# Attention and two feed-forward layers on one core: the opening's hand-written order is replaced, and one product goes to the other PSUM bank

## The chip, the core and the metric

The kernel runs on one core of a Trainium2 chip. The metric is the device time of one execution in microseconds (us); of several runs the median is taken. The core has five engines, each with its own queue of instructions that it works off in order: TensorE (PE; its weight loads stand in the profile as PEld), VectorE (DVE), ScalarE (ACT), GpSimd (POOL) and SyncE (SP), which here only issues DMA transfers.

## What is computed

Three stages, all in float32:

```python
for c in range(24):                                # chunks of 32 queries, 4 batches x 8 heads, head width 64
    k_full = concat(mem_k, k[16 before ... 8 after])   # 8 + 56 keys
    scores = scale * (q_c @ k_full.T)
    a = exp(scores - max); a = a / (sum(a) + 1e-9)
    out[:, :, c] = a @ v_full
x = out as 3072 tokens x 512
h = x @ w_in                                       # 512 x 2048
x = (relu(h) ** 2) @ w_out                         # 2048 x 512
return (silu(x @ w_gate) * (x @ w_val)) @ w_out2   # 512 x 1536 twice, 1536 x 512
```

## The kernel before

**Units and blocks.** Attention is cut into 24 units of 128 queries (4 chunks) with all 8 heads. Four units make a block of 512 tokens, and the first feed-forward layer runs over six such blocks, 16 slices f of its 2048 inner columns in each. For each block and f, PE makes 12 matmuls of the hidden product (L362, from x and w into one of the two PSUM banks `hbank`), ACT and DVE turn them into the squared relu, split into a high part gh and a low part gl, and PE makes 12 matmuls of the projection (L406, into four banks `yb`). The second layer follows with a fast matrix product scheme (L596, L643). Nothing of that is touched.

**The opening.** Until the main loop starts at f = 14 of the first block, the order of all engines is written out by hand: the string `OPENING` is a list of tokens, a letter and a number, and the loop after L760 calls the letter's function with the number. A token may issue instructions on several engines. Since each engine works in order, the sequence of the tokens sets the order in each engine's queue, that of SP's loads too. Waits between engines come from the tiles that the instructions share. The letters that the text below uses, u being a unit and f a slice of weights:

| token | function | engine | what it does |
|---|---|---|---|
| Q u, V u, L f | `at_load`, `at_load_v`, `load1` | SP | load q and k (592 KB), v (512 KB for units 0 to 3), weights (1024 KB) |
| S u | `at_scores` L150 | PE | 32 small score matmuls into bank `yb` (even u) or `abank` (odd u) |
| M, D, A, I, N u | L162, L169, L179, L233/L234, L183 | DVE | max, subtract, sum, reciprocal, scale |
| E u | `at_exp_0` L175 | ACT | exponential |
| T u | `at_turn_0` L189 | PE | 4 transposes of the probabilities |
| C u | `at_turned_0` L192 | ACT | copies them out of PSUM |
| O u | `at_pv_0` L204 | PE | 32 small matmuls, product with v, into `hbank` |
| X u, Y u | L281, L285 | ACT, DVE | high and low part of the unit's 128 columns of x, read from `hbank` |
| p, z or s, j, h, l f | L331, L340 or L335, L345, L349, L353 | ACT, ACT or DVE, DVE, ACT, DVE | turn the loaded weights into a high and a low part |
| x0, y0, w0, v0 | L362 | PE | hidden product of slice 0: x0, y0, w0 for units 0 to 2 (384 columns), v0 for unit 3 |
| a, b f; c, d f | L362; L406 | PE | hidden product; projection |
| Z n | `stir` L753 | PE | n matmuls of a zero tile (`calm`) into `hbank[0]`; nobody reads their result |

The units 0 to 3 have a way of their own (the functions that end in `_0`): there the product with v writes four 128-column pieces into one bank of `hbank`,

```python
o = hbank[1][:, 0:KD * GQ].rearrange("p (j q) -> p j q", q=GQ)
```

so that the product of the next unit (O of u+1) waits until X and Y of unit u have read that bank. x0 writes `hbank[0]` and needs X of units 0, 1 and 2. SP has eight semaphores for its transfers and gives them out in turn, so that the ninth load waits until the first has landed.

Of the kernel before, what the change touches and what calls it, by code (L numbers as in the profile page):

```python
# [20 lines left out]
GQ = NC * CHUNK  # L21
# [5 lines left out]
KD = DM // 128  # L27
# [29 lines left out]
WC = 1024  # L57
EARLY = (1, 2, 3, 4)
OPENING = """
Q0 Z9 S0 M0 D0 Q1 Z1 S1 M1 D1 Q2 Z1 S2 E0 A0 I0 N0 Z7 T0 E1 C0 A1 I1 N1 Q3 S3 L0 p0 T1 C1 M2 D2 M3 D3 E2 A2 I2 V0 Z2 O0 X0 L2  # L60
Y0 V1 Z2 O1 z0 N2 j0 L1 p2 Z6 T2 E3 A3 V2 z2 X1 I3 Y1 N3 C2 s1 p1 Z2 O2 j1 h0 Z4 T3 V3 X2 x0 Y2 C3 O3 l0 j2 y0 h1 L4 p4 X3
h2 l1 Q4 S4 w0 Y3 v0 z4 L3 a1 b1 L5 L6 M4 F4 r0 l2 j4 a2 p3 s3 j3 b2 q0 r1 L7 t0 s5 g0 L8 G4 K4 c0 h3 d0 q1 l3
h4 l4 a3 b3 c1 t1 g1 U4 z6 r2 Q5 p5 j5 s7 q2 V4 p6 t2 r3 h5 L9 q3 d1 a4 L15 b4 c2 g2 d2 a5 j6 r4 l5 t3 g3 b5
W4 c3 s9 h6 l6 p7 j7 L11 d3 O4 s15 p8 z8 j8 r5 S5 M5 L10 q4 q5 a6 p9 b6 c4 t4 g4 d4 h7 l7 a7 t5 L13 g5 b7 c5
F5 j9 h8 l8 G5 r6 K5 d5 a8 X4 b8 Y4 U5 q6 c6 Q6 r7 t6 V5 g6 W5 S6 p10 z10 j10 h9 s11 d6 q7 r8 t7 a9 q8 p11 l9
h10 O5 g7 M6 t8 j11 L12 X5 l10 b9 F6 h11 V6 Y5 G6 g8 c7 l11 d7 a10 K6 U6 b10 r9 z12 q9 p12 j12 t9 g9 c8 d8 p13
a11 W6 s13 b11 c9 d9 L14 r10 O6 z14 h12 Q7 l12 j13 S7 M7 r11 q10 Q8 p14 t10 g10 q11 t11 g11 h13 F7 G7 a12 j14
h14 b12 c10 r12 q12 l13 K7 X6 d10 a13 t12 b13 c11 d11 l14 U7 r13 q13 g12 t13 a14 b14 c12 p15 d12 r14 Y6 q14 W7
j15 h15 V7 O7 S8 t14 a15 X7 l15 b15 g13 c13 M8 Y7 d13 r15 q15 t15 g15 F8 g14
"""  # L70


# [1 line left out]
def attention_moe_moe_kernel(ctx, tc, att, av, v0, w1, w2, out):  # L74
# [19 lines left out]
    hbank = [ps.tile([128, 512], F32, name=f"hbank{i}") for i in range(2)]  # L94
# [99 lines left out]
    def at_pv_0(u):  # L194
        s = st[u]
        v = s["v"].rearrange("p (c j d) -> p c j d", c=NC, d=D)
        o = hbank[1][:, 0:KD * GQ].rearrange("p (j q) -> p j q", q=GQ)
        s["o"] = o.rearrange("p (r i) q -> p r i q", r=2)
        for j in range(NI):
            for c in range(NC):  # L200
                q = slice(32 * c, 32 * c + 32)
                for b in range(2):
                    half = slice(D * b, D * b + D)
                    pe.matmul(  # L204
                        o[half, j, q], v[half, c, j], first_t[u % 2][half, j, q],
                        start=True, stop=True, tile_position=(D * b, D * b),
                    )
# [362 lines left out]
    s3 = []  # L570
# [281 lines left out]
    for k in range(2):  # L852
# [7 lines left out]
        o = acc["x"][:, k:k + 1]  # L860
# [75 lines left out]
```

## Time and profile before

| | us |
|---|---|
| median of 3 runs | 1118.83 (1118.21 to 1119.39) |
| the profiled execution | 1117.84 |
| its span, first to last instruction | 1115.9 |
| around the span | 1.94 |
| PE busy | 1107.7 (99% of the span) |
| DVE, ACT, POOL busy | 657.5, 505.7, 315.9 |
| first projection matmul (c0, L406) starts | 40.65 |

Times inside an execution are counted from the start of its span. In a row of the timeline stand start, length, engine, line, operation, what is written and read, and how many instructions were merged; in square brackets the idle time of the engine before it and what ended it ("issue": nothing that the profile shows). A 32-matmul token has 64 records on PE, since each small float32 matmul is two. PE's clock has two levels, 1.2 and 2.4 GHz; the column PEclk is the granted share of the higher.

### The profile page before, as it was taken

The numbers are of one execution on the slowest core, as the hardware profiler recorded it, in microseconds if no ns is written. First come the engines' busy times: TensorE is split into PE (matmuls) and PEld (weight loads), VectorE is DVE, ScalarE is ACT, GpSimd is POOL, SyncE is SP. The second block draws the span as 40 slices with busy tenths as digits, with TensorE's granted clock in tenths as the row PEclk, the third lists the DMA queues.
The fourth block names the chain that finished last, engine by engine and source line by source line (L and its number), as shares of the span: only waits on it lengthen the run. The fifth ranks groups of instructions, "written<-read, shape, count | busy, mean of one in ns | idle before, by whom it ended". The sixth has DMA issues, their size and how long they took to land.

```text
span 1115.9 us, 17938 instructions
## 1 busy us (share of the span) xinstructions
PE 1107.7 (99%) x7066; PEld 913.5 (82%) x7066; DVE 657.5 (59%) x956; ACT 505.7 (45%) x1026; POOL 315.9 (28%) x261
## 2 busy tenths in 40 slices
PE   8999999999999999999999999999999999999998
PEld 6888888888888888888888888888888888888887
DVE  6879454555454454441523666796666697666664
ACT  4878556556656645553542221452222352222242
POOL 0000025315522521450000332451332461333251
PEclk9999999999999999999999999999999999999999
DMA  9923156656664644634225564457556567655751
GB/s 381 369 78 107 52 201 226 204 206 206 217 219 159 195 153 159 224 127 143 76 76 205 211 231 158 162 210 258 189 205 247 193 208 245 201 200 197 264 208 57
DMA packets 69203, 212.83 MB, mean 191 GB/s; under 512 B 5376, under 2 KB 37632, under 8 KB 52864
## 3 DMA queue, kind: packets, MB, share of 16 engines
q1 hardware_dynamic: 69120, 211.70, 54.4%
q8 instruction: 55, 0.90, 0.3%
q14 instruction: 28, 0.23, 0.1%
HBM read 166.07 MB, written 45.61 MB: 190 GB/s over the span
## 4 chain that ended last, share of the span: by engine, by line
PE 98%; DVE 2%; issue 0%; ACT 0%; DVEq 0%; ACTq 0%
PE yb L406 24%; PE hbank L362 24%; PE hbank L596 15%; PE yb L596 15%; PE yb L643 7%; PE abank L643 7%; PE abank L265 2%; PE abank L150 1%; PE hbank L753 1%; PE hbank L643 1%; PE hbank L204 1%; DVE ring L104 0%; DVE first_p L169 0%; DVE first_p L183 0%; DVE mx L162 0%; DVE sm L179 0%
## 5 line engine op out<-in xcount | busy, mean ns | idle before, releaser
L362 PE MATMUL hbank<-x,w 128*128 128x512 f32 (+2 forms) x1164 | 278.4, 388 | 0.0
L362 PEld LDWEIGHTS hbank<-x,w 128*128 128x128 f32 x1164 | 217.0, 188 | 44.6
L387 DVE TENSOR_TENSOR gl<-r,gh 128x512 fp32r<-128x512 f32 x96 | 75.7, 791 | 246.9 <-ACT r L381 246.8
L406 PE MATMUL yb<-gh,w 128*128 128x512 f32 x768 | 194.7, 392 | 0.0
L406 PEld LDWEIGHTS yb<-gh,w 128*128 128x128 f32 x768 | 142.9, 188 | 30.5
L104 POOL TENSOR_TENSOR ring<-uf,ring 128x512 fp32r<-128x512 f32 x51 | 72.5, 1422 | 294.8 <-ACT ring L101 293.1
L596 PE MATMUL hbank<-w,wst 128*128 128x512 f32 x540 | 132.6, 389 | 0.0
L596 PE MATMUL yb<-w,wst 128*128 128x512 f32 x540 | 132.6, 389 | 0.0
L370 ACT ACTIVATE r<-hbank 128x512 f32<-128x512 f32 x96 | 57.5, 599 | 158.9 <-PE hbank L362 158.9
L461 POOL TENSOR_TENSOR wraw<-cut 128x256 f32<-128x256 f32 x36 | 26.5, 737 | 337.8 <-DVE cut L447 285.4
L596 PEld LDWEIGHTS yb<-w,wst 128*128 128x128 f32 x540 | 101.4, 188 | 21.1
L596 PEld LDWEIGHTS hbank<-w,wst 128*128 128x128 f32 x540 | 101.4, 188 | 21.0
L406 PE MATMUL yb<-gl,w 128*128 128x512 f32 x384 | 105.7, 389 | 0.0
L634 ACT ACTIVATE tmp<-tmp 128x512 f32<-128x512 f32 x36 | 22.8, 632 | 169.4 <-DVE tmp L633 169.4
L583 POOL TENSOR_TENSOR uf<-uf 128x512 f32<-128x512 f32 x36 | 53.9, 1498 | 121.2 <-DVE uf L635 108.0
L101 ACT CAST ring<-uf 128x512 fp32r<-128x512 f32 x108 | 67.0, 621 | 46.1 <-PE yb L643 21.3
L406 PEld LDWEIGHTS yb<-gl,w 128*128 128x128 f32 x384 | 72.0, 188 | 15.0
L643 PE MATMUL yb<-ring,wst 128*128 128x512 f32 x360 | 83.3, 389 | 0.4 <-DVE sum L674 0.4
L643 PE MATMUL abank<-ring,wst 128*128 128x512 f32 x360 | 83.3, 389 | 0.1
L643 PEld LDWEIGHTS yb<-ring,wst 128*128 128x128 f32 x360 | 67.5, 188 | 14.8 <-ACT w L101 0.8
L643 PEld LDWEIGHTS abank<-ring,wst 128*128 128x128 f32 x360 | 67.5, 188 | 14.5 <-issue 0.5
L248 DVE STREAM_TRANSPOSE pT<-prob 32x256 f32<-32x256 f32 x160 | 69.6, 435 | 2.3
(134 smaller groups left out, 1446.1 us busy)
## 6 DMA issues: line engine op xcount, KB each, us to landing
wst<-w2d SPq DMA_DIRECT2D x93, 1024.0 KB, 4.9
wraw<-in_w_dram SPq DMA_DIRECT2D x34, 1024.0 KB, 9.0
w2d<-wraw SPq DMA_DIRECT2D x48, 256.0 KB, 2.5
qk<-in_att_dram SPq DMA_DIRECT2D x20, 592.0 KB, 6.1
v<-in_av_dram SPq DMA_DIRECT2D x20, 384.0 KB, 5.6
y1d<-ys SPq DMA_DIRECT2D x6, 1024.0 KB, 5.3
w2d<-wraw SPq DMA_DIRECT2D x12, 512.0 KB, 3.4
zraw<-y1d SPq DMA_DIRECT2D x6, 1024.0 KB, 7.6
```

The source lines that it names most:

```text
L101: act.copy(hi, src)
L104: lo_engine.tensor_tensor(lo, src, hi.bitcast(F32), ALU.subtract)
L248: dve.transpose(pT[row + k:row + k + 32, pair, :, row:row + 32], probs[u % 2][32 * c:32 * c + 32, :, k:k + 32],)
L362: pe.matmul(hbank[f % 2][:, cols], wt[:, k * 128:(k + 1) * 128], x[:, k, cols], start=i == 0, stop=i == 3 * KD - 1,)
L370: act.activation(r, hbank[f % 2][:, 0:n], AF.Relu)
L387: dve.tensor_tensor(gl, g["r"], g["gh"].bitcast(F32), ALU.subtract)
L406: pe.matmul(ybank[e][:, 0:nt_of[t]], wt[:, c:c + 128], gtile[t, f][g], start=f == 0 and p == 0, stop=f == NF1 - 1 and p == 2,)
L461: pool.tensor_tensor(o, x, y, op)
L583: pool.tensor_tensor(u_of(p, o), u_of(p, x), u_of(p, y), op)
L596: pe.matmul(to, wt[:, k * 128:k * 128 + 128], x[:, k], start=m == 0, stop=m == 5)
L634: act.activation(u4, u4, AF.Silu)
L643: pe.matmul(to[k], wt[:, 128 * k:128 * k + 128], u, start=p == 0 and m == 0, stop=p == NP - 1 and m == 2,)
```

## The change

The string `OPENING` is written anew, in one sequence for all engines, and `at_pv_0` puts the product of unit 1 into `hbank[0]`. Of the zero-tile matmuls 24 are left of 34. The core of the diff (of the string, its first two lines):

```diff
 OPENING = """
-Q0 Z9 S0 M0 D0 Q1 Z1 S1 M1 D1 Q2 Z1 S2 E0 A0 I0 N0 Z7 T0 E1 C0 A1 I1 N1 Q3 S3 L0 p0 T1 C1 M2 D2 M3 D3 E2 A2 I2 V0 Z2 O0 X0 L2
-Y0 V1 Z2 O1 z0 N2 j0 L1 p2 Z6 T2 E3 A3 V2 z2 X1 I3 Y1 N3 C2 s1 p1 Z2 O2 j1 h0 Z4 T3 V3 X2 x0 Y2 C3 O3 l0 j2 y0 h1 L4 p4 X3
...
+Q0 Z9 S0 M0 Q1 V0 Q3 Q2 S1 Z6 M1 D0 S2 E0 D1 A0 I0 E1 A1 N0 I1 M2 N1 L0 S3 T0 p0 Z2 T1 D2 M3 E2 C0 D3 A2 Z3 O0 z0
+X0 j0 I2 N2 Y0 V1 L2 Q4 L1 V2 V3 p2 C1 Z4 T2 S4 O1 E3 A3 I3 N3 h0 C2 p1 X1 s1 j1 Y1 T3 O2 C3 X2 x0 Y2 z2 h1 O3
...
@@
     def at_pv_0(u):
         s = st[u]
         v = s["v"].rearrange("p (c j d) -> p c j d", c=NC, d=D)
-        o = hbank[1][:, 0:KD * GQ].rearrange("p (j q) -> p j q", q=GQ)
+        o = hbank[int(u != 1)][:, 0:KD * GQ].rearrange("p (j q) -> p j q", q=GQ)
```

On PE, from the scores of unit 1 on. `hbank_74` and `hbank_75` are `hbank[0]` and `hbank[1]`, `yb_77` and `abank` hold scores, `yb_78` and `yb_79` the transposes of even and odd units. Before:

```order
L753 MATMUL hbank_74<-calm 128x512
L150 MATMUL yb_77<-early 32x64 x32
L753 MATMUL hbank_74<-calm 128x512 x7
L189 MATMUL yb_78<-eye,first_p 128x128 x4
L150 MATMUL abank<-early 32x64 x32
L189 MATMUL yb_79<-eye,first_p 128x128 x4
L753 MATMUL hbank_74<-calm 128x512 x2
L204 MATMUL hbank_75<-first_p,first_v 64x32 x32
L753 MATMUL hbank_74<-calm 128x512 x2
L204 MATMUL hbank_75<-first_p,first_v 64x32 x32
L753 MATMUL hbank_74<-calm 128x512 x6
L189 MATMUL yb_78<-eye,first_p 128x128 x4
```

Now:

```order
L753 MATMUL hbank_74<-calm 128x512 x6
L150 MATMUL yb_77<-early 32x64 x32
L150 MATMUL abank<-early 32x64 x32
L189 MATMUL yb_78<-eye,first_p 128x128 x4
L753 MATMUL hbank_74<-calm 128x512 x2
L189 MATMUL yb_79<-eye,first_p 128x128 x4
L753 MATMUL hbank_74<-calm 128x512 x3
L204 MATMUL hbank_75<-first_p,first_v 64x32 x32
L753 MATMUL hbank_74<-calm 128x512 x4
L189 MATMUL yb_78<-eye,first_p 128x128 x4
L150 MATMUL abank<-early 32x64 x32
L204 MATMUL hbank_74<-first_p,first_v 64x32 x32
```

The scores of units 2 and 3 now stand side by side ahead of the first transposes; the transposes of unit 2 and the scores of unit 4 stand ahead of the product of unit 1, which goes to the other bank; and from there to O3 no zero-tile matmul is left.

On ACT, from the two first exponentials on. Before:

```order
L175 ACTIVATE first_p<-first_p 128x512 x2
L192 COPY first_p<-yb_78 128x512
L331 ACTIVATE wraw<-wraw 128x1024
L192 COPY first_p<-yb_79 128x512
L175 ACTIVATE first_p<-first_p 128x512
L281 CAST x_339<-hbank_75 128x4x128
```

Now:

```order
L175 ACTIVATE first_p<-first_p 128x512 x2
L331 ACTIVATE wraw<-wraw 128x1024
L175 ACTIVATE first_p<-first_p 128x512
L192 COPY first_p<-yb_78 128x512
L340 ACTIVATE wraw<-wraw 128x1024
L281 CAST x_337<-hbank_75 128x4x128
```

C0, the copy that O0 waits for (L192 from `yb_78`), moved behind p0 (L331, which waits for the weights of L0) and E2.

On SP, the first loads (`qk` and `early` are q and k of units 0 to 4, `first_v` is v, `wraw` are weights):

```order
 L129 DMA qk<-in_att_dram 128x1184
-L129 DMA early<-in_att_dram 128x1184 x3
+L129 DMA early<-in_att_dram 128x1184
+L137 DMA first_v<-in_v_dram 128x1024
+L129 DMA early<-in_att_dram 128x1184 x2
 L323 DMA wraw<-in_w_dram 128x2048
 L137 DMA first_v<-in_v_dram 128x1024
 L323 DMA wraw<-in_w_dram 128x2048
-L137 DMA first_v<-in_v_dram 128x1024
+L129 DMA early<-in_att_dram 128x1184
```

The v of unit 0 moved from sixth to third place, q and k of unit 2 from third to fifth (the string says Q3 Q2), the first weights from fifth to sixth, q and k of unit 4 from thirteenth to ninth.

## Rows read from the trace of the kernel before

**Rows 1.** The page: busy time and instructions by engine, and one DMA queue.

```profile
PE 1107.7 (99%) x7066; PEld 913.5 (82%) x7066; DVE 657.5 (59%) x956; ACT 505.7 (45%) x1026; POOL 315.9 (28%) x261
...
q8 instruction: 55, 0.90, 0.3%
```

**Rows 2.** Waits of PE from 30 us to the end, longest first.

```profile
PE yb L643 <- DVE sum L674: 0.4, 1, 0.4
```

**Rows 3.** Timeline of PE in the opening.

```profile
7.17 0.86 PE L150 MATMUL abank<-early 64*32 64x64 f32 x64
...
9.45 1.85 PE L753 MATMUL hbank<-calm 128*128 128x512 f32 x7
...
12.46 1.03 PE L150 MATMUL abank<-early 64*32 64x64 f32 x64
...
14.63 2.05 PE L204 MATMUL hbank<-first_p,first_v 64*64 64x32 f32 x64
...
18.68 2.29 PE L204 MATMUL hbank<-first_p,first_v 64*64 64x32 f32 x64 [1.33 <-DVE first_p L183]
20.91 2.93 PE L753 MATMUL hbank<-calm 128*128 128x512 f32 x6
...
28.39 0.94 PE L362 MATMUL hbank<-x,w 128*128 128x384 f32 x4
29.36 2.06 PE L204 MATMUL hbank<-first_p,first_v 64*64 64x32 f32 x64
31.35 0.97 PE L362 MATMUL hbank<-x,w 128*128 128x384 f32 x4
32.25 0.86 PE L150 MATMUL abank<-early 64*32 64x64 f32 x64
33.04 7.77 PE L362 MATMUL hbank<-x,w 128*128 128x384 f32 x40
40.65 1.98 PE L406 MATMUL yb<-gh,w 128*128 128x512 f32 x8
```

**Rows 4.** Timeline of DVE: Y0, then N2.

```profile
17.40 0.65 DVE L285 TENSOR_TENSOR x<-hbank,x 128x512 fp32r<-128x512 f32 x1
17.96 0.68 DVE L183 TENSOR_TENSOR first_p<-first_p,sm 128x512 f32<-128x512 f32 x1
```

**Rows 5.** Busy time in stretches: PE, PEld, DVE, ACT, POOL, then PEclk, DMA share, GB/s.

```profile
0.00:12.52 12.52, 10.20 (x218) 7.24 (x223) 5.83 (x14) 2.75 (x4) 1.62 (x8) 1.00 0.86 333
0.00:17.36 17.36, 14.94 (x350) 10.88 (x350) 10.32 (x25) 6.23 (x10) 1.62 (x8) 1.00 0.91 360
...
17.36:18.64 1.28, 0.00 (x0) 0.00 (x0) 1.28 (x4) 1.28 (x2) 0.00 (x0) 1.00 0.92 384
20.40:23.70 3.30, 3.30 (x19) 2.55 (x17) 2.50 (x6) 1.11 (x2) 0.00 (x0) 0.50 1.03 418
```

**Rows 6.** Timeline of PEld inside the scores of unit 3.

```profile
12.46 0.54 PEld L150 LDWEIGHTS abank<-early 64*32 64x32 f32 x40 [0.17 <-issue]
```

**Rows 7.** DMA queue q8 in two stretches: 10.3:11.4 and 16.2:17.3.

```profile
q8 instruction: 1, 0.02, 5.3%
...
q8 instruction: 1, 0.02, 5.9%
```

**Rows 8.** DMA issues at 0.80 (Q0), 2.19 (Q3), 3.45 (V0): KB, us to landing.

```profile
qk<-in_att_dram SPq DMA_DIRECT2D x1, 592.0 KB, 4.1
...
early<-in_att_dram SPq DMA_DIRECT2D x1, 592.0 KB, 7.0
...
first_v<-in_v_dram SPq DMA_DIRECT2D x1, 512.0 KB, 10.4
```

**Rows 9.** Timeline of ACT: p0, E2, X2.

```profile
13.05 1.16 ACT L331 ACTIVATE wraw<-wraw 128x1024 f32<-128x1024 f32 x1
...
15.02 0.63 ACT L175 ACTIVATE first_p<-first_p 128x512 f32<-128x512 f32 x1 [0.16 <-DVE first_p L169]
...
27.12 0.59 ACT L281 CAST x<-hbank 128x512 fp32r<-128x512 f32 x1 [0.19 <-PE hbank L204]
```

More of the change, by code (lines that the diff above doesn't have):

```diff
@@ L59 @@
 OPENING = """
-Q0 Z9 S0 M0 D0 Q1 Z1 S1 M1 D1 Q2 Z1 S2 E0 A0 I0 N0 Z7 T0 E1 C0 A1 I1 N1 Q3 S3 L0 p0 T1 C1 M2 D2 M3 D3 E2 A2 I2 V0 Z2 O0 X0 L2
-Y0 V1 Z2 O1 z0 N2 j0 L1 p2 Z6 T2 E3 A3 V2 z2 X1 I3 Y1 N3 C2 s1 p1 Z2 O2 j1 h0 Z4 T3 V3 X2 x0 Y2 C3 O3 l0 j2 y0 h1 L4 p4 X3
[L62 to L69, printed above, removed]
+Q0 Z9 S0 M0 Q1 V0 Q3 Q2 S1 Z6 M1 D0 S2 E0 D1 A0 I0 E1 A1 N0 I1 M2 N1 L0 S3 T0 p0 Z2 T1 D2 M3 E2 C0 D3 A2 Z3 O0 z0
+X0 j0 I2 N2 Y0 V1 L2 Q4 L1 V2 V3 p2 C1 Z4 T2 S4 O1 E3 A3 I3 N3 h0 C2 p1 X1 s1 j1 Y1 T3 O2 C3 X2 x0 Y2 z2 h1 O3
+l0 j2 y0 L4 X3 p4 Y3 M4 l1 w0 v0 a1 b1 L3 L7 z4 h2 r0 p3 s3 l2 a2 r1 q0 j3 q1 t0 g0 L8 L5 L6 h3 F4 G4 t1 s7 l3
+s5 j4 b2 c0 h4 p5 r2 d0 a3 b3 c1 K4 g1 Q5 L9 L15 L10 V4 L12 l4 j5 r3 q2 q3 t3 t2 h5 z6 p6 d1 a4 g3 g2 U4 c2 b4
+d2 a5 l5 W4 r4 p8 j6 b5 p7 z8 q4 h6 r5 j7 l6 O4 j8 S5 c3 d3 L13 Q6 c4 a6 h7 q5 t4 g4 s15 M5 s9 F5 l7 d4 a7 b7
+b6 c5 G5 h8 p9 t5 p10 r6 K5 U5 g5 l8 a8 d5 X4 b8 j9 W5 Y4 q6 c6 t6 L11 V5 g6 S6 h9 r7 p11 s11 M6 q7 r8 a9 O5
+d6 t7 z10 F6 j10 l9 h10 q8 g7 j11 L14 Q7 X5 l10 h11 t8 G6 g8 c7 b9 d7 a10 K6 l11 U6 r9 z12 p12 q9 j12 t9 g9 Y5
+W6 s13 b10 c8 d8 r10 a11 b11 c9 h12 p13 q10 z14 V6 l12 j13 S7 O6 r11 p14 t10 q11 h13 t11 g10 M7 F7 G7 a12 d9
+j14 g11 c10 d10 b12 r12 h14 q12 l13 K7 a13 t12 X6 b13 a14 c11 g12 l14 U7 r13 p15 q13 b14 d11 c12 d12 t13 r14
+W7 j15 Y6 q14 h15 V7 Q8 O7 S8 c13 t14 X7 a15 g13 M8 l15 b15 d13 Y7 g14 r15 q15 t15 g15 F8
 """
```

## The prediction

> **What bounds the kernel now.** I read the page first: PE is busy for 1107.7 of 1115.9 us [rows 1], so the time falls only by what PE stands still for, does for nothing, or does at the lower clock. Then PE's waits: from 30 us to the end there are 0.4 us of them [rows 2]. The change can therefore act only in the first 33 us, and one number measures it: when c0, the first projection matmul, starts (40.65 now [rows 3]). Before it PE has the same real work in both orders, and from the matmuls at 33.04 on it has no gap. Third, the timeline of PE up to there [rows 3] against those of DVE and ACT [rows 4, 9]. Last the DMA queues [rows 7, 8], because the loads are reordered too.
>
> Two things in the opening are not what they seem. **O1** is shown as waiting 1.33 us for N2 [rows 3], but it reads nothing of N2; it needs bank 1 free from Y0, which ends at 17.40 + 0.65 = 18.05 [rows 4], and still starts at 18.68. Between 17.36 and 18.64 PE issues no weight load either [rows 5]. Up to there it had issued 350 + 350 = 700 instructions [rows 5]. It stood once before with nothing to wait for, 0.17 us inside the scores of unit 3, which took 1.03 instead of 0.86 [rows 3, 6], after 218 + 223 = 441 [rows 5]. The distance is 259. Queue q8, named "instruction", brings 55 packets of 0.90 MB, one for 2 x 7066 / 55 = 257 PE instructions [rows 1], and a packet ended about 1.3 us before each of the two stands [rows 7]. So I read: PE stood for its code, a block of some 256 instructions at a time, and while the loads fill the DMA engines the block after next comes one trip after PE enters the next one. The trips: the boundary at 441 - 256 = 185 lies 0.25 us into S1 (Z9, S0 and one zero matmul are 148 instructions), at 7.4, and PE went on at 12.7: 5.3 us; from there to 18.65: 5.9 us.
>
> By the Trainium skill, page "Runtime: NRT & Kernel Launch", section "Instruction fetch mechanics", code comes in 16 KiB blocks of 256 instructions, and a block boundary is "mostly hidden". The blocks agree with the rows; the hiding does not, in 17.36 to 18.64.
>
> The other thing is **the clock**: from 20.4 to 23.7 it was at 0.50, 1.2 GHz [rows 5], after the pause and the thin matmuls of O1. Six zero matmuls took 2.93 us there, against 1.85 for seven at the full clock [rows 3].
>
> **The change, part by part.** I lay the new order out with the row durations.
>
> *Loads.* Q0 lands at 4.9, Q3 at 9.2 [rows 8], 1.44 us a load of 592 KB; 512 KB by size 1.25. S1 can go right after S0 at 6.8 (now 7.17, one zero matmul less). Q2 is fifth instead of third, behind V0 and Q3: it lands at 9.2 + 1.25 = 10.5 instead of 7.8, and S2 goes to 10.5 to 11.3. S1 ends at 7.65 and the six zero matmuls (6/7 of 1.85 [rows 3]) at 9.2; 1.3 us of pause remain. S3 follows and is cut by the first code boundary: 185 instructions lie 0.25 us into S1, at 7.05, plus 5.3 is 12.35. S3 ends near 12.9, which is 0.6 earlier than now. L0 comes after the same bytes as V0 does now and lands at 3.45 + 10.4 = 13.85 [rows 8].
>
> *O0.* On ACT, C0 is queued behind p0, which waits for L0, and behind E2: 13.85 + 1.05 + 0.55 + 0.6 (ACT's instructions overlap their neighbours by 0.1) [rows 9] puts its end at 16.0. O0 starts at 16.0 instead of 14.63, with 0.8 us of pause after the three zero matmuls. It takes 2.0 [rows 3], and the four zero matmuls end at 19.1. T2 and S4, which now stands at 32.25, follow by 20.75; DVE has a weight join (j0) queued ahead of the N2 that T2 waits for, and half a us there changes nothing, since the code sets the end of O1, as follows.
>
> *O1, other bank.* It no longer waits for Y0, and O2 no longer for X1 and Y1. x0, which writes that bank, now waits for Y1 as well, but it needs X2 anyhow, which is later. O1 starts at 20.75, and here the code decides. The boundaries after 441 and 700 lie at 956 and 1212. Counted through the new order, 700 falls into the four zero matmuls, 956 into O1 with 12 of its 128 instructions left, at 22.5. The blocks come at 12.35, then 18.3 and 24.3, with 5.9 to 6.0 us a trip. So O1 stands for 1.9 us at its end and is done at 24.6. With the short trip of 5.3 twice it would stand 0.5 us; with half a us more each, 2.9.
>
> *To c0.* T3 0.4; O2 25.05 to 27.05; X2 0.6 [rows 9], a pause of 0.7; x0 at 27.75 instead of 28.39; O3 needs Y2 (0.65 like Y0 [rows 4]) and runs from 28.65 to 30.65 (31.35 now); the next 256 run out 0.4 us before its end, at 30.25, when their block is just due (24.3 + 5.9). y0 takes 0.7, and since S4 (32.25 to 33.04) is already done, the long run of 40 matmuls starts at 31.35 instead of 33.04. **Order alone: -1.7 us.** The ten zero matmuls less cost or give nothing of their own: they lay in pauses, and the pauses that are left (1.3, 0.8, 1.9, 0.7) are longer than now.
>
> *After c0.* The same matmuls follow in another order, 1.7 us earlier. With the row durations no wait of PE comes out up to 130 us; the nearest is 0.2 us of room at the product with v of unit 4, near 78 us. The loads that fill the DMA engines until 50 us are the same bytes. I cost this at 0, with 0.2 to 1 us if that room is gone.
>
> *The clock.* Now no zero matmul stands between 19.1 and x0. The stretch from 20.75 to 27.75 has O1, 1.9 us of stand, O2 and 0.7 us of pause; the stretch ahead of the fall at 20.4 had O0's end, two zero matmuls, 1.3 us of stand and O1. I take one stretch of 3.3 us at 0.50 in it or behind it. Its price lies between 0 (all on pauses) and half of it, 1.65 (all on wide matmuls: 0.26 each at full, 0.49 at half clock [rows 3]). O1 lost 2.29 - 2.05 = 0.24 us with about 0.6 us of it in the low stretch [rows 3, 5], a loss of 0.4 a us. With 2.0 us on O2 or O3, 0.6 on pause and 0.7 on x0 I get 0.8 + 0.3 = **+1.1 us**.
>
> **The sum**: -1.7 + 1.1 = -0.6 us against the profiled execution, 1117.2. The median of the runs is 0.99 above that execution; I let the new one have the same: **1118.2**.
>
> **Rivals.** *One: PE does not stand for code in O1.* Either the trips are as short as the first or my reading of 18.68 is wrong. By that page's rule this is what happens. The sum that follows needs only the rows: O1 ends at 22.75, T3 at 23.2, O2 at 25.2, x0 starts at 25.9, O3 at 26.75, and the 40 matmuls at 29.4: -3.6 us, 1114.2 in the profiled measure, 1115.2 as a median; with one low stretch 1116.3. For it: only two stands show. Against it: both lie 256 instructions apart, and nothing else is due then. Chance 0.17.
>
> *Two: the clock stays down, and the kernel is slower.* With no zero matmuls from 19.1 on, nothing dense comes until 31; now six at half clock stood right behind the fall, and the clock was back at 23.8. If it stays at 0.50 from about 23.7 to 34, three stretches cost 1.1 + 1.1 + 1.65 = 3.85, and -1.7 + 3.85 = +2.1, 1120.9; with code later by 0.5 us a trip, 1.0 us in all, 1121.9. With two stretches, +0.5, 1119.3, it is still no change. It decides from the third stretch on. Chance of three 0.12, of two 0.18.
>
> *Three: the gain is lost behind c0.* Weights or the unit-4 product come as late as before, and PE waits there: 1118.8. Against it: no wait comes out of the durations. Chance 0.08. That the change is not made as told can be left out: the new order stands in the program's queues.
>
> **The numbers.** A difference of 0.2%, 2.24 us, is about what a measurement of this kernel can tell from no change. The forecast (0 or 1 low stretch, 1117.1 to 1118.2) has 0.45. Faster, under 1116.6, are most of rival one and a little of the forecast: 0.18. Slower, over 1121.07, is most of rival two with three stretches: 0.1. The rest, 0.72, is within. The range goes from rival one with a small part of a low stretch, 1115.6, to three stretches, cut a little, 1120.8.
>
> **What would show it.** Right: S2 starts near 10.5; O0 near 16; O1 starts near 20.75 and is drawn out to 3.5 us or more, with a packet on q8 ending 1.3 us ahead of its rest; c0 starts between 39 and 40; one low stretch of the clock between 20 and 31; no wait of PE after 40. Wrong: O1 in 2.1 us (rival one), the clock at 0.50 still at 32 (rival two), or c0 early and a PE wait of a us or more between 40 and 130 (rival three).

## The result, and the profile after

| | before | after |
|---|---|---|
| median (range) of 6 runs each, side by side | 1118.47 (1117.85 to 1119.39) | 1124.34 (1122.98 to 1126.30) |
| the profiled execution | 1117.84 | 1124.26 |
| its span | 1115.9 | 1122.4 |
| c0 starts | 40.65 | 47.10 |
| profiled execution less c0 | 1077.19 | 1077.16 |

The ratio is 1.0053, with a 95% interval of 1.0040 to 1.0066: slower by half a per cent, beyond the range that was given. The last line of the table says where: whatever stands behind c0 takes the same time to 0.03 us, and c0 itself comes 6.45 us late. The waits of PE from 30 us to the end agree; only x0 has one now that it did not have (in the kernel before it ran at 28.39, behind zero matmuls and T3). Behind it stands the one that was there before [rows 2], and no other:

```profile
PE hbank L362 <- ACT x L281: 0.7, 1, 0.7
PE yb L643 <- DVE sum L674: 0.4, 1, 0.4
```

So the view to read is again the timeline of PE in the opening. To be held against [rows 3]:

```profile
7.08 1.66 PE L753 MATMUL hbank<-calm 128*128 128x512 f32 x6
10.39 0.85 PE L150 MATMUL yb<-early 64*32 64x64 f32 x64 [1.65 <-DVE sm L233]
11.04 0.36 PE L150 MATMUL abank<-early 64*32 64x64 f32 x15
12.69 0.97 PE L150 MATMUL abank<-early 64*32 64x64 f32 x49 [1.28 <-issue]
...
16.01 0.95 PE L753 MATMUL hbank<-calm 128*128 128x512 f32 x3
16.89 2.06 PE L204 MATMUL hbank<-first_p,first_v 64*64 64x32 f32 x64
...
20.44 0.86 PE L150 MATMUL abank<-early 64*32 64x64 f32 x64
21.23 1.87 PE L204 MATMUL hbank<-first_p,first_v 64*64 64x32 f32 x57
24.85 0.42 PE L204 MATMUL hbank<-first_p,first_v 64*64 64x32 f32 x7 [1.75 <-issue]
25.20 0.66 PE L189 MATMUL yb<-eye,first_p 128*128 128x128 f32 x4
25.79 3.31 PE L204 MATMUL hbank<-first_p,first_v 64*64 64x32 f32 x64
29.78 1.65 PE L362 MATMUL hbank<-x,w 128*128 128x384 f32 x4 [0.68 <-ACT x L281]
31.36 3.63 PE L204 MATMUL hbank<-first_p,first_v 64*64 64x32 f32 x64
34.92 12.34 PE L362 MATMUL hbank<-x,w 128*128 128x384 f32 x44
47.10 1.98 PE L406 MATMUL yb<-gh,w 128*128 128x512 f32 x8
```

Up to 25 us this is the layout of the prediction. O1 stands for 1.75 us with 57 of its 64 records done, on "issue", which is nothing that the profile shows. Queue q8 had one packet ahead of it (22.3 to 23.5):

```profile
q8 instruction: 1, 0.02, 5.7%
```

Then the same instructions begin to take longer. O3 lasts 3.63 us where it lasted 2.06 [rows 3], x0 1.65 instead of 0.94. The view by stretches gives the reason in its PEclk column (columns as in [rows 5]):

```profile
0.00:12.54 12.54, 8.23 (x222) 6.09 (x223) 6.23 (x17) 2.75 (x4) 1.62 (x8) 1.00 0.85 335
12.54:15.96 3.42, 3.27 (x58) 2.80 (x58) 2.12 (x5) 1.91 (x3) 0.00 (x0) 0.50 1.02 424
15.96:26.20 10.24, 8.49 (x224) 7.23 (x224) 8.08 (x15) 7.35 (x11) 0.00 (x0) 1.00 1.03 419
26.20:43.26 17.06, 16.38 (x154) 15.07 (x151) 9.02 (x11) 8.13 (x10) 0.00 (x0) 0.50 1.01 417
43.26:60.00 16.74, 16.74 (x75) 13.86 (x74) 12.17 (x18) 14.26 (x34) 0.00 (x0) 1.00 0.69 231
```

Before, the granted clock was at 0.50 once, from 20.3 to 23.7. Now it is so from 12.5 to 16.0 and again for 17 us, from 26.2 to 43.3. PE is not idle there: it is busy for 16.38 of 17.06 us. Within that stretch most of the 44 matmuls of the long run, y0 among them, went on at half clock (here the instructions of L362 alone: PE, PEld, then PEclk, DMA share, GB/s; an instruction that runs across a bound is counted on both sides):

```profile
34.92:40.20 5.28, 5.28 (x21) 5.28 (x21) 0.50 1.01 413
40.20:43.26 3.06, 3.06 (x9) 2.38 (x9) 0.50 1.02 423
43.26:47.10 3.84, 3.84 (x18) 2.98 (x16) 1.00 1.04 374
```

They are of three widths (L362 alone, from 34.9 to 47.2): first the eight of y0 and w0 with 384 columns, then the twelve of v0 with 128, then those with 512.

```profile
L362 PE MATMUL hbank<-x,w x44: 308/415/735, 34.9 to 46.9; 128*128 128x512 f32 x24, 128*128 128x128 f32 x12, 128*128 128x384 f32 x8
```

**What the clock cost.** From the start of O2 to c0 the changed kernel took 47.10 - 25.79 = 21.31 us. At the full clock the same work takes: O2 1.99 (as O3 did, 29.36 to 31.35) and the pause for X2 0.68; then from x0 to c0, as before but without S4, 40.65 - 28.39 - (33.04 - 32.25) = 11.47 [rows 3]. Together 14.14. From O2 on the clock cost 7.2 us by this sum. All that stands ahead of O2, the low stretch at 12.5 included, gained the rest, 7.2 - 6.45 = 0.7 us. More than half of the 7.2 us lies in the long run: from 34.92 to c0 it took 12.18 us, where the same 44 matmuls took 0.90 + 7.61 = 8.51 before [rows 3].

### The profile page after: what moved, and what is told of

It is laid out like the page before. It is cut to its first block, busy times and chain, and to the rows that moved or that the text cites. A ratio compares the mean times of both kernels' runs of the same rounds, so it can differ in the third digit from the quotient of the medians.

```text
span 1122.4 us, 17926 instructions
## 1 busy us (share of the span) xinstructions
PE 1111.3 (99%) x7056; PEld 918.3 (82%) x7056; DVE 657.4 (59%) x956; ACT 505.8 (45%) x1026; POOL 316.2 (28%) x261
## 4 chain that ended last, share of the span: by engine, by line
PE 98%; DVE 1%; issue 0%; ACT 0%
PE hbank L362 24%; PE yb L406 24%; PE yb L596 15%; PE hbank L596 15%; PE yb L643 7%; PE abank L643 7%; PE abank L265 2%; PE abank L150 2%; PE hbank L204 1%; PE hbank L643 1%; PE hbank L753 1%; DVE ring L104 0%; PE yb L189 0%; PE yb L150 0%; DVE mx L162 0%
## 5 line engine op out<-in xcount | busy, mean ns | idle before, releaser
L362 PE MATMUL hbank<-x,w 128*128 128x512 f32 (+2 forms) x1164 | 282.8, 393 | 0.7 <-ACT x L281 0.7
L362 PEld LDWEIGHTS hbank<-x,w 128*128 128x128 f32 x1164 | 221.1, 192 | 45.7 <-ACT x L281 0.8
```

Source lines behind the costliest of these rows:

```text
L362: pe.matmul(hbank[f % 2][:, cols], wt[:, k * 128:(k + 1) * 128], x[:, k, cols], start=i == 0, stop=i == 3 * KD - 1,)
```

## The experiments

Theory A: the time went into the clock, which stayed low because from O1 to the long run PE has no zero matmuls any more, only narrow ones, x0 and pauses. Theory B: the order itself (the loads, C0 behind p0 and E2, the stand for code) lost the time, and the clock only shows it. In the diffs a piece of `OPENING` stands alone; B n is a new token, n zero matmuls into `hbank[1]` where Z writes `hbank[0]`. Every kernel was timed beside the kernel before on the same chip (there 1118.94 to 1119.34).

| run | median (range) | ratio [95%] | profiled | c0 | clock at 0.50, 7 us to c0 |
|---|---|---|---|---|---|
| zeros back | 1118.92 (1118.10 to 1119.99) | 0.9995 [0.9985, 1.0004] | 1118.96 | 41.67 | none |
| early zeros only | 1123.64 (1122.85 to 1127.68) | 1.0053 [1.0036, 1.0071] | 1122.85 | 45.75 | 25.5 to 39.1 |
| eight zeros ahead of x0 | 1122.63 (1120.55 to 1123.13) | 1.0031 [1.0019, 1.0042] | 1121.09 | 43.92 | 12.7 to 16.0, 26.4 to 33.1 |
| before, less Z6 | 1120.19 (1118.06 to 1120.92) | 1.0004 [0.9995, 1.0014] | 1119.72 | 42.31 | 20.1 to 30.2 |
| S4 back | 1119.73 (1118.13 to 1120.96) | 1.0005 [0.9996, 1.0014] | 1120.02 | 42.79 | 11.7 to 15.0, 28.7 to 35.5 |
| zeros back, S4 back | 1118.15 (1117.39 to 1120.35) | 0.9992 [0.9983, 1.0001] | 1120.35 | 43.19 | 20.9 to 24.2 |
| bank alone | 1119.04 (1117.97 to 1119.84) | 1.0004 [0.9995, 1.0013] | 1119.11 | 41.91 | 18.1 to 24.8 |
| zeros back, bank undone | 1118.85 (1118.30 to 1128.54) | 1.0014 [0.9996, 1.0033] | 1118.30 | 41.14 | none |
| S4 back, zeros, first | 1118.18 (1117.12 to 1123.68) | 1.0005 [0.9990, 1.0020] | 1117.12 | 39.95 | none |
| S4 back, zeros, second | 1117.37 (1117.07 to 1124.12) | 0.9997 [0.9984, 1.0010] | 1117.17 | 39.97 | none |
| S4 back, zeros, third | 1117.39 (1117.04 to 1118.17) | 0.9983 [0.9974, 0.9993] | 1117.38 | 40.25 | none |

In all of them the profiled execution less c0 is 1077.10 to 1077.41, so c0 is the one number to compare. It differs between executions of one kernel, since the clock does not fall at the same place in each; one profile shows one of them.

### Zero matmuls put back (changed kernel)

```diff
-S1 Z6 M1
+S1 Z11 M1
-Z3 O0
+Z6 O0
-T2 S4 O1 E3
+T2 S4 Z4 O1 B5 E3
-O2 C3 X2 x0
+O2 C3 X2 Z4 x0
```

> The changed kernel with zero-tile matmuls put back into its pauses and nothing else moved: 11 instead of 6 ahead of S2, 6 instead of 3 ahead of O0, 4 ahead of O1, 5 behind O1 (into hbank[1], which is free there), 4 ahead of x0. Theory A (the time went into the clock, which stood at 0.50 from 26.2 to 43.3 because nothing dense stands between 19.9 and 35): no stretch at 0.50 between 7 us and the end, c0 near 40.5 instead of 47.1, and a median of 1117.5 to 1118.5, level with the kernel before. Theory B (the new order, its loads and its stand for code lose the time, and the clock is a side effect): the 18 more matmuls cost 18 x 0.26 = up to 4.7 us where they don't lie in a pause, c0 at 47 or later and 1124 to 1129.

The clock did not fall at all (all engines, then PEclk):

```profile
7.00:41.67 34.67, 31.25 (x565) 26.36 (x549) 24.46 (x43) 20.95 (x29) 0.00 (x0) 1.00 1.02 419
```

Eighteen useless matmuls were added and the 0.5% is gone: 0.9995 instead of 1.0053. Theory B, which had 1124 or more, falls. c0 came 1.2 us later than expected, and the median lies 0.4 us above the expected range. The stand in O1 is still there, shorter because O1 starts later:

```profile
22.57 1.52 PE L204 MATMUL hbank<-first_p,first_v 64*64 64x32 f32 x45
25.07 0.77 PE L204 MATMUL hbank<-first_p,first_v 64*64 64x32 f32 x19 [0.97 <-issue]
```

### More zero matmuls in the early pauses alone (changed kernel)

```diff
-S1 Z6 M1
+S1 Z12 M1
-T0 p0 Z2 T1
+T0 p0 Z4 T1
-Z3 O0
+Z7 O0
```

> The changed kernel with more zero matmuls in the early pauses alone: 12 instead of 6 ahead of S2, 4 instead of 2 between T0 and T1, 7 instead of 3 ahead of O0. From T2 to x0 nothing is added. Theory A: the stretch at 0.50 from 12.5 to 16 goes away, the long one behind O1 stays, because its cause is the stand for code in O1 and the thin work up to x0: c0 45 to 48, 1122 to 1126. If any zero matmuls at all mended it, 1119.

```profile
7.00:25.50 18.50, 14.91 (x359) 12.40 (x359) 15.00 (x32) 9.56 (x13) 0.00 (x0) 1.00 1.02 420
25.50:39.10 13.60, 12.91 (x150) 11.90 (x147) 6.13 (x9) 6.68 (x9) 0.00 (x0) 0.50 1.01 419
```

As theory A has it: the first low stretch is gone, the long one is not, and the ratio is that of the changed kernel. Zero matmuls ahead of O0 do not bring it back; the place that matters lies behind them.

### Eight zero matmuls ahead of x0 (changed kernel)

```diff
-O2 C3 X2 x0
+O2 C3 X2 Z8 x0
```

> The changed kernel with one edit: eight zero matmuls ahead of x0, where PE pauses 0.7 us for X2. At half clock they take about 3.9 us, so 3.2 us of useless work in the way. Theory A (the clock comes back behind dense work, whoever reads it): it comes back at about 33 to 34 instead of 43.3, c0 at 42.5 to 44.5 instead of 47.1, and the time falls by 2 to 4 us against the changed kernel, to 1120 to 1122. Theory B (the clock is a side effect, or dense work does not bring it back): 3.2 us later, 1127 or more.

```profile
24.88 0.42 PE L204 MATMUL hbank<-first_p,first_v 64*64 64x32 f32 x7 [1.85 <-issue]
25.82 3.24 PE L204 MATMUL hbank<-first_p,first_v 64*64 64x32 f32 x64
28.98 3.78 PE L753 MATMUL hbank<-calm 128*128 128x512 f32 x8
32.56 1.13 PE L362 MATMUL hbank<-x,w 128*128 128x384 f32 x4
33.62 2.06 PE L204 MATMUL hbank<-first_p,first_v 64*64 64x32 f32 x64
...
43.92 1.98 PE L406 MATMUL yb<-gh,w 128*128 128x512 f32 x8
```

```profile
26.40:33.10 6.70, 6.70 (x62) 5.86 (x59) 3.29 (x4) 2.75 (x4) 0.00 (x0) 0.50 1.02 421
33.20:43.92 10.72, 10.72 (x112) 9.46 (x111) 5.89 (x8) 7.64 (x11) 0.00 (x0) 1.00 1.02 419
```

The stand in O1 ends where it did (24.88, and 24.85 in the changed kernel), so the zero matmuls are all that differs behind it. The fall is where it was, at 26.4, and 3.8 us of work that nobody reads bring the clock back at 33.1 instead of 43.3. c0 comes 3.2 us earlier than in the changed kernel; the time's interval moves from 1.0040 to 1.0066 down to 1.0019 to 1.0042; the median, 1122.63, is a little above the 1120 to 1122 expected. Theory B expected 3.2 us later.

### The kernel before without Z6

```diff
-L1 p2 Z6 T2
+L1 p2 T2
```

> The kernel before without its six zero matmuls behind O1 (Z6, 20.91 to 23.84 at half clock), nothing else. Theory A: they were what brought the clock back at 23.7; without them it stays at 0.50 beyond 30, c0 at 41 to 45 instead of 40.65 though 2.9 us of useless work are gone, and the median is 1119 to 1123. Theory B: useless work in the way is gone, c0 1 to 1.5 us earlier, 1117 to 1117.5.

```profile
20.10:30.20 10.10, 10.10 (x115) 8.83 (x113) 6.10 (x10) 4.59 (x6) 0.00 (x0) 0.50 1.02 419
```

The converse, in the old order: without its six zero matmuls the low stretch lasts 10.1 us instead of 3.4, and c0 comes at 42.31 although 2.9 us of useless work are gone (O1 started 0.4 us later in this execution, at 19.09). The median lies 0.85 us above that of the kernel before, within what the interval can tell from nothing; theory B's gain of 1 to 1.5 us did not come. The six zero matmuls paid for themselves; that they gave more is not shown.

### S4 back behind y0 (changed kernel)

```diff
-T2 S4 O1
+T2 O1
-y0 L4 X3
+y0 S4 L4 X3
```

> The changed kernel with one token moved: S4 (the scores of unit 4) back behind y0, where the kernel before has it. No zero matmul is added. It moves 128 PE instructions out of the way of O1, so that the 956th falls into O2 or ahead of it and not into O1. Theory of the code stand: O1 runs through in 2.0 to 2.1 us at the full clock, and the stand, what is left of it, moves into T3 or O2 (about 0.5 us or none); the real work up to x0 is 1 to 2 us earlier. Theory A: the pauses stay without dense work, the clock falls again between 20 and 27 and stays at 0.50 for 10 us or more, so 1121 to 1125; were the clock to stay up, c0 would be at 38 and the median at 1116. Theory B: S4 ahead of O1 is the loss, and its move gives 5 us back, 1118 to 1119, with the clock still low.

```profile
19.61 0.85 PE L753 MATMUL hbank<-calm 128*128 128x512 f32 x3 [0.36 <-issue]
20.30 0.60 PE L189 MATMUL yb<-eye,first_p 128*128 128x128 f32 x4
21.01 2.06 PE L204 MATMUL hbank<-first_p,first_v 64*64 64x32 f32 x64
...
24.01 1.70 PE L204 MATMUL hbank<-first_p,first_v 64*64 64x32 f32 x52
26.54 0.54 PE L204 MATMUL hbank<-first_p,first_v 64*64 64x32 f32 x12 [0.82 <-issue]
```

O1 runs through, and the stand has moved on into O2, 12 records from its end: the boundary stays with the count of instructions and not with the token. The clock still falls, but for 6.8 us, from 28.7 to 35.5, and the time is level with the kernel before:

```profile
28.70:35.50 6.80, 6.80 (x135) 6.13 (x135) 3.27 (x4) 4.16 (x6) 0.00 (x0) 0.50 1.01 419
```

That is below the 1121 of theory A and above the 1119 of theory B. So moving S4 alone, without one more zero matmul, took back most of the loss (1.0005 against 1.0053). What it changed is again mostly the length of the low stretch, 6.8 us against 17. Whether the shorter stand (0.82 against 1.75 us) or S4's new place behind y0 did that was not separated.

### The price of the stand: zeros back, S4 back

The first run of this section with the S4 edit of the run above and the same zero matmuls.

> The run with zero matmuls put back (11, 6, 4, 5, 4) and one more edit: S4 behind y0. It prices the stand for code in O1 at the full clock. Theory of the code stand: S4 ahead of O1 costs the stand it makes (0.97 us in that run's trace) and nothing else, since its own 0.8 us are only moved: O1 unbroken at 2.06 us, c0 0.8 to 1.2 us earlier than there (41.67), median 1117.8 to 1118.2. If PE did not stand for code there, moving S4 changes nothing: c0 at 41.7.

The profile fell on the slowest of ten executions, and it cannot give the price: there the code came late for O0,

```profile
16.52 1.87 PE L204 MATMUL hbank<-first_p,first_v 64*64 64x32 f32 x57
19.89 0.42 PE L204 MATMUL hbank<-first_p,first_v 64*64 64x32 f32 x7 [1.50 <-issue]
```

and the clock fell behind it, though O1 ran unbroken (2.06 us). The medians, 1118.15 against 1118.92, differ by 0.8 us the way that was expected, but the intervals of the two ratios overlap (0.9983 to 1.0001 and 0.9985 to 1.0004), so the price of the stand is not shown.

### The bank

In the kernel before, the bank change alone, with the zero matmuls between O1 and O2 sent to the other bank:

```diff
-o = hbank[1][:, 0:KD * GQ].rearrange("p (j q) -> p j q", q=GQ)
+o = hbank[int(u != 1)][:, 0:KD * GQ].rearrange("p (j q) -> p j q", q=GQ)
-p2 Z6 T2
+p2 B6 T2
-p1 Z2 O2
+p1 B2 O2
```

> The kernel before with the bank change alone: the product of unit 1 in hbank[0], and the eight zero matmuls between it and the product of unit 2 in hbank[1], so that they don't wait for its readers. By the reading of the prediction the product of unit 1 stood for code until 18.6, not for the reader of bank 1, which ended at 18.05: it starts at 18.6 to 18.7 as before, c0 within 0.3 us of the kernel before, ratio within 0.9995 to 1.0005. If the bank was what it waited for, it starts 0.6 us earlier.

The reader Y0 of the old bank (DVE), then O1 (PE):

```profile
17.04 0.69 DVE L285 TENSOR_TENSOR x<-hbank,x 128x512 fp32r<-128x512 f32 x1 [0.42 <-ACT x L281]
```

```profile
18.71 3.63 PE L204 MATMUL hbank<-first_p,first_v 64*64 64x32 f32 x64 [1.68 <-ACT wraw L340]
```

O1 starts at 18.71 as before (18.68 [rows 3]), 0.98 us after Y0's end, though it no longer waits for Y0. What the timeline puts the wait down to has nothing to do with O1: a weight tile now, N2 before. Nor was it the v of unit 1, which O1 also reads and which the prediction left out. That load was issued at 4.42 in the kernel before and landed 13.2 us later, at 17.6 (4.49 and 13.1 here):

```profile
first_v<-in_v_dram SPq DMA_DIRECT2D x1, 512.0 KB, 13.2
```

O1 started 1.1 us after that, while S2, where the profile has it wait for its load, started 0.1 us after the landing (11.9 and 12.02 in the run with S4 back). This supports the reading that O1 stood for code. The ratio, 1.0004, has an interval that takes in no change. But c0 came at 41.91, 1.3 us later than in the profile of the kernel before and not within 0.3 as expected: the clock was low for 6.7 us here, against 3.4, and O1 ran in it:

```profile
18.10:24.80 6.70, 6.08 (x70) 5.56 (x71) 4.23 (x8) 3.10 (x4) 0.00 (x0) 0.50 1.02 414
```

The converse, in the kernel with the zeros back (`hbank[1]` again, and Z5 for B5):

> The run with zero matmuls put back (11, 6, 4, 5, 4 of them, S4 left where the change has it), with the bank change undone: the product of unit 1 in hbank[1] again, the five behind it into hbank[0]. The product of unit 2 then waits for X and Y of unit 1, about 1.3 us behind the end of O1 (26.0 + 1.3 = 27.3 in the other run), where it started at 27.57 anyway: both banks come out the same within 0.3 us, 1118 to 1119. If the bank change is worth something here, PE shows a wait of 0.5 us or more at the product of unit 2 and the time goes up by as much.

O2 started at 27.03 with no wait in front of it, behind its T3. Six of ten executions lie between 1118.30 and 1118.86, three at 1120 to 1121, and one at 1128.54 with a mean clock of 0.991, so the interval is wide. A gain from the bank change is not shown.

### A version faster than both

Both edits together, S4 behind y0 and zero matmuls in the pauses, three times with other counts (ahead of S2, between T0 and T1, ahead of O0, behind O0, ahead of O1, behind O1, ahead of x0): 11, 2, 6, 4, 2, 4, 3.

> Both edits: S4 behind y0, and zero matmuls in the pauses (11 ahead of S2, 6 ahead of O0, 2 ahead of O1, 4 behind O1 into hbank[1], 3 ahead of x0). Theory A with the code stand: no stretch at 0.50 between 7 us and the end, no stand of over 1 us inside O1, c0 near 39.0, that is 1.6 us ahead of the kernel before (40.65), and a median of 1116.5 to 1117.3. Theory B: as the run with S4 moved alone, or later by what the added matmuls take.

Seven of the ten executions took 1117.1 to 1118.7, only the fastest of them within the 1116.5 to 1117.3 that was expected of the median; three took 1122.3 to 1123.7 at a mean clock of 0.995 to 0.997. c0 was at 39.95 in the profile, 1 us later than expected. Then 10, 2, 5, 7, 0, 5, 3:

> The version with S4 behind y0 and zero matmuls, their places evened out: 10 ahead of S2, 5 ahead of O0, 7 behind O0 and none ahead of O1, 5 behind O1, 3 ahead of x0. In the earlier version 7 of 10 executions took 1117.1 to 1118.7 and 3 took 1122.3 to 1123.7 with a lower mean clock. [...] Expected: no execution over 1120.5, median 1117.3 to 1118.0, c0 at 39.2 to 39.9, ratio 0.998 to 0.999. [...]

Eight of ten at 1117.1 to 1118.2, but one at 1120.1 and one at 1124.1: the expectation that none would be left was wrong. Then 12, 4, 7, 7, 0, 4, 3:

```diff
-S1 Z6 M1
+S1 Z12 M1
-T0 p0 Z2 T1
+T0 p0 Z4 T1
-Z3 O0
+Z7 O0
-C1 Z4 T2 S4 O1 E3
+C1 Z7 T2 O1 B4 E3
-O2 C3 X2 x0
+O2 C3 X2 Z3 x0
-y0 L4 X3
+y0 S4 L4 X3
```

> The version with S4 behind y0 and zero matmuls in every pause: 12 ahead of S2, 4 between T0 and T1, 7 ahead of O0, 7 behind O0, 4 behind O1, 3 ahead of x0. Two of ten executions of the version with 10, 2, 5, 7, 5, 3 still lost 3 and 7 us to the clock. With the early pauses filled I expect c0 at 39.3 to 40.0 in every execution, the median at 1117.0 to 1117.8, none over 1119.5, ratio 0.998 to 0.999. If executions of 1122 or more remain, the thin matmuls of O0 with their stand are enough by themselves to bring the clock down, and zeros around them don't mend it.

```profile
21.61 2.06 PE L204 MATMUL hbank<-first_p,first_v 64*64 64x32 f32 x64
23.60 1.19 PE L753 MATMUL hbank<-calm 128*128 128x512 f32 x4
24.63 0.60 PE L189 MATMUL yb<-eye,first_p 128*128 128x128 f32 x4
25.15 2.06 PE L204 MATMUL hbank<-first_p,first_v 64*64 64x32 f32 x64
```

```profile
7.00:40.25 33.25, 31.69 (x586) 26.69 (x574) 25.07 (x44) 20.88 (x29) 0.00 (x0) 1.00 1.02 418
```

All ten executions lie between 1117.04 and 1118.17, all at a mean clock of 0.999 or 1.000; the ratio is 0.9983 [0.9974, 0.9993]. From O1 to O2 PE is without a gap; c0, at 40.25, came a little later than the 39.3 to 40.0 expected. It beats the kernel before by 0.17%, where the changed kernel, at 1.0053, lost 0.5%. How much of that is the order and how much the clock is not shown. In the two profiles c0 is only 0.4 us earlier (40.25 against 40.65), with no low stretch here and one of 3.4 us there, while the medians are 1.9 us apart: the kernel before had mean clocks of 0.996 to 0.998 in its executions. The old order with all its pauses filled was not run.

## Why the prediction was wrong, and where it was right

**Right: what measures it.** c0 did measure the whole change: behind it both kernels take 1077.2 us, and no wait of PE was added after 40 us, so rival three falls.

**Right: the loads and the code.** S2 started at 10.39 (forecast 10.5). S3 was cut by the first boundary and went on at 12.69 (12.35). O1 started at 21.23 (20.75); its block came at 24.85 (24.3), with 7 of 64 records left (forecast 12 of 128 instructions, which is 6 records); the stand was 1.75 us (1.9). Rival one falls with it. By the Trainium skill, page "Runtime: NRT & Kernel Launch", section "Instruction fetch mechanics", a boundary is "mostly hidden". While the loads fill the DMA engines (a share of 1.03 from 16.0 to 26.2), it is not: 1.28 and 1.75 us in this one execution, and 0.97, 0.82 and 1.50 us in others above. That it follows the count of instructions was shown by moving S4. One row was misread on the way: the 0.17 us in brackets in [rows 6] lie ahead of the scores, and that as much was lost inside them follows only from 1.03 against 0.86.

**Short: the order alone.** Forecast -1.7, and -0.7 is what is left once the clock's 7.2 us are taken out. 0.74 us of the difference is that O2 started at 25.79 instead of 25.05. The rest is in the sum itself: it put x0 at 0.9 and y0 at 0.7 us, where [rows 3] have 0.97 and 0.90 from start to start. O0 had been late too, at 16.89 instead of 16.0. C0 was in time, by ACT's timeline,

```profile
15.74 0.57 ACT L192 COPY first_p<-yb 128x512 f32<-128x512 f32 x1
```

ending at 16.31. It was PE that came late, with zero matmuls at half clock (16.01 above), in a low stretch from 12.5 that was not foreseen; ahead of it lay the pauses of 1.65 and 1.28 us with thin matmuls between them. Whether O1's block would have come sooner without that stretch is not settled: in the run with early zeros alone the stretch was gone, and PE went on at 24.84 all the same, but its added zero matmuls had O0 start hardly sooner (16.75).

**Wrong: the step "I take one stretch of 3.3 us at 0.50 ... +1.1 us".** The price was 7.2 us, because the stretch behind O1 lasted 17 us and not 3.3. The price of one us in it was right: 7.2 of 17.06 is 0.42, and the forecast had read 0.4 off O1. What failed is the length. Two readings led there. First, that the ten zero matmuls less "cost or give nothing of their own: they lay in pauses". The rows showed what six of them did at 20.91 to 23.84: the clock was back right behind them. The prediction named this under rival two and gave it a chance of 0.30 in all. Taking six away from the old kernel let its low stretch grow from 3.4 to 10.1 us; putting eight into the new one shortened its long one from 17 to 6.7.

Second, the end of the stretch. Even rival two, with the right mechanism, let the clock return at 34; its dearest case was 1121.9. It did not count that work takes longer at half clock (O3 3.63 us instead of 2.06) and so keeps PE longer under it. Above all it had the long run at the full clock, and that alone lost 3.7 us: 21 of its matmuls (eight of 384 columns, twelve of 128, one of 512) started from 34.92 to 40.20 without bringing the clock back, and seven more of 512 before it came. A loss of that kind feeds itself, and a rival that rests on it needs a much longer tail than "two or three stretches" priced one by one.

**Rival two** was the right one, then, with the wrong size. The sign of the change was set by how long the clock stayed low behind the stand for code. Eight zero matmuls behind it shorten that, and so does S4 in its old place. The bank and the loads show no part in it: with both as the change has them and zero matmuls put back, the time is level with the kernel before.

## What to carry to other kernels

Work that nobody reads can be worth its time when it stands where PE pauses or runs thin matmuls: before taking it out, look at the granted clock right behind it, and ask what will bring the clock back without it. When such a stretch is forecast, do not take the length that it had before: lay the work behind it out at half-clock durations, the wide matmuls too, and give it a long tail. In an opening where the loads fill the DMA engines, count PE's instructions too: a token of 128 moved ahead of a critical one can put a block boundary into it.

## What was not expected of the hardware

- PE can be busy for 16.38 of 17.06 us and still be granted 0.50. What preceded the returns differs: six zero matmuls in the kernel before, eight in the run with eight; y0, S4 and the first of the long run in the run with S4 back; 28 matmuls of the long run, 8.3 us of it, in the changed kernel, but only 3.1 us of the same run (36.0 to 39.1) in the one with early zeros; and at 16.0 in the changed kernel scores, transposes and two zero matmuls. What decides it stays open.
- In the changed kernel the clock fell behind pauses no longer than 1.75 us, between thin matmuls (32 or 64 columns), and not always: ten executions of one kernel had mean clocks from 0.995 to 1.000, worth 7 us (1117.1 to 1124.1). What decides it between executions of the same instructions stays open.
- The block that PE stands for came up to 1.4 us apart in executions of kernels that are the same up to there, 57 records into O0: PE went on at 18.51 with the bank undone, 18.75 with the zeros back, and 19.89 with S4 back besides.
